# Retention and FFN on one core: four more tiles turned by DMA, mask products and state sums moved to later slots, and the first states kept in their own output bank

## The chip, the core and the metric

The kernel runs on one core of a Trainium2 chip. The metric is the device time of one execution in microseconds (us), shown as the median of several runs. The engines are named as in the profile: PE is the matrix engine (PEld its weight loads), DVE the vector engine, ACT the scalar engine, POOL the general engine (GpSimd), SP the engine that here only issues DMAs. SBUF is the on-chip memory, PSUM the accumulator memory of eight banks.

## The reference, cut to what matters

```python
# q, k, v: (8 batches, 8 heads, 576 positions, 64); w_in (512, 2048); w_out (2048, 512)
scores = scale * np.matmul(q, k.transpose(0, 1, 3, 2))
Dmat = np.where(rel >= 0, gamma[:, None, None] ** rel[None, :, :], 0.0)   # rel = i - j
attn = np.matmul(scores * Dmat[None], v)
x = attn.transpose(0, 2, 1, 3).reshape(8 * 576, 512)
h = x @ w_in
g = np.where(h > 0.0, h, np.exp(np.minimum(h, 0.0)) - 1.0)
out = g @ w_out                                                           # (4608, 512) float32
```

A causal linear attention with a decay per head is followed by a two-layer feed-forward network (FFN) with an ELU between its layers. All matrix products are in bf16 with float32 accumulation.

## The kernel before

The 4608 tokens are cut into 36 units of 128 tokens. Two batches make nine units (`R = 9`); the fifth of each nine holds the end of one batch and the start of the next. The decay factors apart: `gk` scales the rows of v, `gx` the outputs.

**A unit's attention.** `load_v` (SP's queue) and `load_qk` (POOL's queue, cast to bf16 on the way) bring the data in. `scale_v` (POOL) writes `vn`. `turn` makes `qkT`, the transposed q and k: for units below `PE_TURNED = 12` by eight PE transposes into the score bank (tag `sc`), copied out by DVE (q) and ACT (k); from unit 12 on by one DMA transpose from SBUF to SBUF on SP's queue. `scores` (PE, L211) fills the score bank, `masks` (DVE, L223) multiplies it with the triangular mask into `pt`. `inter` (L244, queries times the running state `sb`) and `intra` (L299, `pt` times `vn`) build the unit's output in the bank pair `o`, of which there is one. `put_x` (DVE, L312) multiplies it by `gx` and writes `xt`, the input of the FFN. `state` (PE, L260) computes the unit's own contribution k^T v into the unused half of the `o` bank of the unit before; `state_out` (DVE, L275 to L281, then a cast on ACT) adds it to the running sum and makes the next `sb`. For units 0 to 3, `state_aside` (ACT, L290) first copies the contribution out of PSUM, so that the bank is free.

**The FFN.** Units are gathered in groups of 1 to 4. `ffn1` (L382) makes one 512-wide bank `ph` (three banks, tag `ph`); ACT takes its exp (`e`, L387), POOL forms `m = e - 1` (L389), and DVE writes `g` (L347), the step that frees the bank. That last step is held back in the list `late` and written into the program three slots later by `finish`. `ffn2` (L407, in the start L438) multiplies `g` with w_out into `pm`; ACT copies the result and a DMA writes it out.

**Order.** The schedule is manual: every engine runs its instructions in the order in which the program emits them. The start up to unit 5 is written out by hand, with dummy matmuls (`dummy`, L452) between the first units. Then a list of slots, one per `ffn1` or `ffn2` call (four groups of matmuls), is walked; due times place the calls of unit u between them: `stretch(u)` (scores of u+1, inter and intra of u, state of u+1, then the DVE work), `turn`, `scale_v` and the loads. A unit below 12 is turned and scaled about two units ahead of its stretch, a later one three. `todo` holds calls for later slots; `tick` ends each slot.

The emission of DVE's work in `stretch` before:

```python
        if u == 5:
            finish(2)
        if last:
            put_x(u)
        if ahead:
            masks(u + 1)
        if not last:
            put_x(u)
        if ahead:
            todo.append((slot[0] + 1, lambda: state_out(u + 1, True)))
```

Of the kernel before, what the change touches and what calls it, by code (L numbers as in the profile page):

```python
# [9 lines left out]
FP32 = mybir.dt.float32  # L10
# [7 lines left out]
def kernel(  # L18
# [9 lines left out]
    nc = tc.nc  # L28
    PSUM = bass.MemoryType.PSUM

    B, H, S, D = q.shape
    DM, DF = moe_w_in.shape
    P = 128
    HP = H // 2
    KJ = DM // P
    NFT = DF // P
    NU = B * S // P
# [5 lines left out]
    GROUPS += [list(range(u, u + 4)) for u in range(16, NU, 4)]  # L43
    NG = len(GROUPS)
    group_of = {u: (g, i) for g, us in enumerate(GROUPS) for i, u in enumerate(us)}
    PE_TURNED = 12

    def place(u):

# [114 lines left out]
    def make_gx(*hps):  # L164
        for hp in hps:
            nc.scalar.activation(gx[:, hp, :S], px, AF.Exp, bias=bx, scale=lgx[:, hp : hp + 1])


    qkTs, vns, scs, pts, os_, sbs, sts, sums = {}, {}, {}, {}, {}, {}, {}, {}

# [7 lines left out]
            gk[:, u % R, h0:h1].unsqueeze(2).to_broadcast([P, h1 - h0, D]), ALU.mult,  # L178
        )

    def turn(u, bank=None, keys_on_v=False):

        t = tpool.tile([P, 2, HP, P], BF16, name="qkT", tag="qkT")
        n = kns[u]
        c_v = 1 if keys_on_v else 0
        if u < PE_TURNED:
            if bank:
                pool, tag = bank
                ps = [pool.tile([P, HP, P], BF16, name="tr", tag=tag) for c in range(2)]
            else:  # L190
                both = ps_s.tile([P, 2, 2, HP, P], BF16, name="tr", tag="sc")
                ps = [both[:, c, 0] for c in range(2)]
            for c in range(2):
                for hp in range(HP):
                    nc.tensor.transpose(ps[c][:, hp], n[:, c, 2 * hp : 2 * hp + 2].rearrange("p h d -> p (h d)"), ident)  # L195
            nc.vector.tensor_copy(t[:, c_v], ps[c_v])
            nc.scalar.copy(t[:, 1 - c_v], ps[1 - c_v])  # L197
        else:
            nc.sync.dma_start_transpose(
                t.rearrange("p c h t -> p (c h) t"), n.rearrange("p c h d -> p (c h d)")  # L200
            )
        qkTs[u] = t
# [14 lines left out]
    def masks(u, i=None):  # L217

        if u not in pts:
            pts[u] = ppool.tile([P, 2, HP, P], BF16, name="pt", tag="pt")  # L220
        m = mask[:, 1 if u % R == 4 else 0]
        s = slice(0, 2) if i is None else slice(i, i + 1)
        nc.vector.tensor_tensor(  # L223
            pts[u][:, s].rearrange("p i h t -> p (i h) t"), scs[u][:, s].rearrange("p i h t -> p (i h) t"),
            m.unsqueeze(1).to_broadcast([P, (s.stop - s.start) * HP, P]), ALU.mult,
        )
# [4 lines left out]

    def inter(u):

        o = ps_o.tile([P, 2, 512], FP32, name="o", tag="o")
        os_[u] = o
        r = u % R
        if r == 0:
            return
        n = 64 if r == 4 else P
        for a in range(2):  # L240
            for b in range(2):
                for i in range(2):
                    rows = slice(i * D, (i + 1) * D)
                    nc.tensor.matmul(  # L244
                        o[b * D : (b + 1) * D, i, a * P : a * P + n], sbs[u][rows, 2 * b + a],
                        qkTs[u][rows, 0, 2 * b + a, :n],
                        start=(a == 0), stop=False, skip_group_check=True,
                    )

    def state(u):  # L250

        r = u % R
        if r == 8:
            return
        sts[u] = os_[u - 1][:, 1 if r == 4 else 0, 256:512].rearrange("p (c d) -> p c d", c=HP)
        rows = slice(64, P) if r == 4 else slice(0, P)
        for hp in range(HP):
            for i in range(2):
                h = 2 * hp + i
                nc.tensor.matmul(  # L260
                    sts[u][i * D : (i + 1) * D, hp], kns[u][rows, 1, h], vns[u][rows, h],
                    start=(hp == 0), stop=(hp == HP - 1), skip_group_check=True,
                )

    slot = [0]
    todo = []

    def state_out(u, cast_later=False):
        r = u % R
        if r == 8:  # L270
            return
        s = ppool.tile([P, HP, D], BF16, name="sb", tag="sb")
        sbs[u + 1] = s
        if r in (3, 7):
            nc.vector.tensor_tensor(s, sts[u], sums[u - 1], ALU.add)  # L275
            return
        sums[u] = ppool.tile([P, HP, D], FP32, name="sum", tag="sum")
        if r in (0, 4):
            nc.vector.tensor_copy(sums[u], sts[u])
        else:  # L280
            nc.vector.tensor_tensor(sums[u], sts[u], sums[u - 1], ALU.add)  # L281
        if cast_later:
            todo.append((slot[0] + 1, lambda: nc.scalar.copy(s, sums[u])))  # L283
        else:
            nc.scalar.copy(s, sums[u])

    def state_aside(u):

        c = ppool.tile([P, HP, D], FP32, name="stc", tag="stc")
        nc.scalar.copy(c, sts[u])  # L290
        sts[u] = c

    def intra(u):
        o = os_[u]
# [11 lines left out]
    def put_x(u):  # L306
        g, i = group_of[u]
        if i == 0:
            xts[g] = xpool.tile([P, KJ, 512], BF16, name="xt", tag="xt")
        r = u % R  # L310
        s0 = P * r if r < 5 else 64 + P * (r - 5)
        nc.vector.tensor_tensor(  # L312
            xts[g][:, :, i * P : (i + 1) * P].rearrange("p (a i) t -> p a i t", a=2), outputs(os_[u]),
            gx[:, :, s0 : s0 + P].rearrange("p (a i) t -> p a i t", a=2), ALU.mult,
        )

    def stretch(u, ahead=True):

        ahead = ahead and u + 1 < NU
        if ahead:  # L320
            scores(u + 1)
        inter(u)
        intra(u)
        if ahead:
            state(u + 1)
        last = GROUPS[group_of[u][0]][-1] == u
        if u == 5:
            finish(2)
        if last:
            put_x(u)  # L330
        if ahead:
            masks(u + 1)
        if not last:
            put_x(u)
        if ahead:
            todo.append((slot[0] + 1, lambda: state_out(u + 1, True)))


    gts = {}
# [3 lines left out]
    def finish(n=0):  # L343

        while late and late[0][0] <= slot[0] - n:
            _, gt_, ph, m, _ = late.pop(0)
            nc.vector.scalar_tensor_tensor(gt_, ph, 0.0, m, ALU.max, ALU.min)  # L347
# [98 lines left out]

    V, A, G = nc.vector.tensor_copy, nc.scalar.copy, nc.gpsimd.tensor_copy

    def dummy(n, bank=(ps_m, "pm")):
        dum = bank[0].tile([P, 512], FP32, name="dum", tag=bank[1])  # L450
        for _ in range(n):
            nc.tensor.matmul(dum, warm[:, :P], warm, start=True, stop=True)  # L452

    def product(u):
        inter(u)
        intra(u)
        put_x(u)
# [17 lines left out]
    load_w_out(0, 8)  # L475
    load_w_out(8, 16)
    dummy(2)
    os_[-1] = ps_o.tile([P, 2, 512], FP32, name="o", tag="o")
    for u in range(2):
        scores(u)  # L480
        masks(u)
        if u == 0:
            make_gx(1, 2, 3)
        dummy(1)
        state(u)
        state_aside(u)
        dummy(2)
        turn(u + 1, h, True)
        product(u)
        state_out(u)  # L490
        dummy(2)
# [5 lines left out]
    def f1(g, n, bank=None):  # L497
        k = 512 // (P * len(GROUPS[g]))
        ffn1(g, k * n, bank)

    ffn1_part(0, 0, 0, 2)
    state(2)
    state_aside(2)
    ffn1_part(0, 1, 0, 2)
    product(2)
    state_out(2)
# [11 lines left out]
    for n in range(4, 16):  # L518
        f1(0, n, m if n % 4 == 1 else None)
        if n == 9:  # L520
            turn(3)
        if n in (9, 10):
            scale_v(3, n - 9)
        if n == 11:
            scores(3)
            masks(3, 0)
        if n == 12:
            masks(3, 1)
            state(3)
            state_aside(3)  # L530
        if n == 13:
            product(3)
            state_out(3)
    for n in range(4):
        f1(1, n, m if n == 1 else None)
        if n == 0:
            load_v(4, nc.vector)
    load_qk(4)
    finish()
# [12 lines left out]
    load_v(7, nc.vector)  # L552
    ffn2_part(1, 8, 16, None)
    scores(4)
    state(4)
    masks(4)
    state_out(4)
    scale_v(6)
    ffn2_part(2, 8, 16, None)
    product(4)  # L560
    turn(5)
    load_qk(8)
    load_v(8, nc.vector)
    ffn2_part(3, 8, 16, None)
    scores(5)
    state(5)
    masks(5)
    state_out(5)
    f1(2, 0)
    f1(2, 1)  # L570
    turn(6)
    f1(2, 2)
    load_qk(9)
    load_v(9, nc.vector)
# [30 lines left out]
    for u in range(5, NU):  # L605
        def at(share):
            return due[u] + share * (due[u + 1] - due[u])
        events.append((due[u], 0, u))
        if u + 2 < PE_TURNED:
            events += [(due[u], 3, u + 2), (at(0.7 if u in (5, 7) else 0.5), 1, u + 2)]  # L610
        if PE_TURNED <= u + 3 < NU:
            t = at(0.4) if u + 2 < PE_TURNED else due[u]
            events += [(t, 1, u + 3), (t, 3, u + 3)]
        if u + 5 < NU:
            events += [(at(0.25), 4, u + 5), (at(0.6), 5, u + 5)]
    events.sort()
# [50 lines left out]
```

## Time and profile before

| | before |
|---|---|
| median of 12 runs | 314.97 us (314.05 to 316.79) |
| profiled execution | 314.16 us, span 312.4 us |
| PE busy | 302.1 us, 97% |
| DVE, ACT, POOL busy | 183.1, 127.4, 201.8 us |
| granted PE clock | 1.00 |
| DMA | 39.55 MB, mean 127 GB/s |
| DMA transposes on SP | 24, median 4.4 us from issue to landing |
| PE transposes | 96 matmuls, DVE copies 12 x 422 ns, ACT copies 12 x 585 ns |

The span runs from the first to the last instruction of the profiled execution; the rest of the run's own time lies around it. Busy shares are averages over stages; matmuls overlap, so their mean duration is longer than the distance between two of them. The chain of waits follows the work that ended last back to the start, and shows in order of time what each step stood on.

### The profile page before, as it was taken

The numbers are of one execution on the slowest core, as the hardware profiler recorded it, in microseconds if no ns is written. First come the engines' busy times: TensorE is split into PE (matmuls) and PEld (weight loads), VectorE is DVE, ScalarE is ACT, GpSimd is POOL, SyncE is SP. The second block draws the span as 40 slices with busy tenths as digits, with TensorE's granted clock in tenths as the row PEclk, the third lists the DMA queues.
The fourth block names the chain that finished last, engine by engine and source line by source line (L and its number), as shares of the span: only waits on it lengthen the run. The fifth ranks groups of instructions, "written<-read, shape, count | busy, mean of one in ns | idle before, by whom it ended". The sixth has DMA issues, their size and how long they took to land.

```text
span 312.4 us, 7391 instructions
## 1 busy us (share of the span) xinstructions
PE 302.1 (97%) x2925; PEld 166.7 (53%) x2964; DVE 183.1 (59%) x309; ACT 127.4 (41%) x237; POOL 201.8 (65%) x292
## 2 busy tenths in 40 slices
PE   8899999999999999999999999999999999999996
PEld 3475646777765555555444444444444444444444
DVE  4679425767685766765766665666665665434300
ACT  4556314335534443344344433444344433444411
POOL 8887794978987787797777666766664433333300
PEclk9999999999999999999999999999999999999999
DMA  9999999997899999999999999999995200100112
GB/s 156 189 202 206 169 169 216 180 175 56 107 148 190 134 130 151 155 151 163 114 150 137 135 136 134 136 135 136 135 136 86 67 36 35 36 34 34 64 72 70
DMA packets 146659, 39.55 MB, mean 127 GB/s; under 512 B 137600, under 2 KB 142080, under 8 KB 146624
## 3 DMA queue, kind: packets, MB, share of 16 engines
q0 software_dynamic: 77264, 13.64, 55.8%
q1 hardware_dynamic: 67920, 23.14, 39.3%
q10 hardware_dynamic: 1440, 2.29, 2.1%
q8 instruction: 23, 0.38, 0.5%
q14 instruction: 12, 0.10, 0.1%
HBM read 36.70 MB, written 9.44 MB: 148 GB/s over the span
## 4 chain that ended last, share of the span: by engine, by line
PE 86%; DMA 7%; DVE 3%; issue 2%; POOL 1%; ACT 0%; SPq 0%; DVEq 0%; POOLq 0%
PE ph L382 36%; PE pm L407 34%; DMA w_in_sb<-in_moe_w_in_dram 6%; PE pm L438 4%; PE sc L211 4%; PE o L299 4%; DMA rv<-in_v_dram 2%; PE o L260 1%; PE pmh L423 1%; PE o L244 1%; PE tr L195 1%; DVE g L347 1%; DVE pt L223 1%; DVE xt L312 0%; SPq L114 0%
## 5 line engine op out<-in xcount | busy, mean ns | idle before, releaser
L389 POOL TENSOR_SCALAR m<-e 128x512 bf16<-128x512 f32 (+1 forms) x156 | 90.6, 583 | 91.7 <-ACT e L387 87.0
L382 PE MATMUL ph<-xt,w_in_sb 128*128 128x512 bf16 (+3 forms) x792 | 141.5, 312 | 2.7 <-DVE g L347 1.1
L347 DVE SCALAR_TENSOR_TENSOR g<-ph,m 128x512 bf16<-128x512 f32 (+1 forms) x156 | 99.5, 647 | 67.5 <-POOL m L389 67.0
L387 ACT ACTIVATE e<-ph 128x512 f32<-128x512 f32 (+1 forms) x156 | 87.1, 564 | 125.5 <-PE ph L382 119.0
L407 PE MATMUL pm<-w_out_sb,g 128*128 128x512 bf16 x478 | 122.8, 379 | 1.6 <-issue 1.0
L382 PEld LDWEIGHTS <-w_in_sb 128*128 128x128 bf16 x808 | 68.8, 98 | 54.1 <-issue 2.4
L407 PEld LDWEIGHTS <-g 128*128 128x128 bf16 x496 | 47.8, 98 | 53.0 <-issue 0.3
L223 DVE TENSOR_TENSOR pt<-sc,mask 128x1024 bf16<-128x1024 f32 (+1 forms) x37 | 44.1, 1192 | 19.5 <-PE sc L211 18.4
L176 POOL TENSOR_TENSOR vn<-rv,gk 128x512 bf16<-128x512 f32 (+1 forms) x37 | 37.8, 1022 | 0.2 <-DMA rv<-in_v_dram 0.2
L93 POOL DMA_DIRECT2D qkn<-in_q_dram x39 | 35.1, 899 | 0.5 <-issue 0.4
L93 POOL DMA_DIRECT2D qkn<-in_k_dram x39 | 33.4, 858 | 1.0 <-DMA qkn<-in_k_dram 1.0
L312 DVE TENSOR_TENSOR xt<-o,gx 128x512 bf16<-128x512 f32 x36 | 24.7, 685 | 12.1 <-PE o L260 8.3
L414 ACT COPY ot<-pm 128x512 f32<-128x512 f32 x31 | 18.1, 585 | 13.9 <-PE pm L407 13.9
L211 PEld LDWEIGHTS <-qkT 64*64 64x64 bf16 x576 | 9.2, 106 | 13.9 <-issue 10.6
L211 PE MATMUL sc<-qkT 64*64 64x128 bf16 x576 | 15.0, 222 | 0.6 <-ACT qkT L197 0.2
L299 PE MATMUL o<-pt,vn 128*64 128x128 bf16 x288 | 14.9, 225 | 0.1
L438 PE MATMUL pm<-w_out_sb,g 128*128 128x512 bf16 x61 | 14.2, 379 | 0.2
L197 ACT COPY qkT<-tr 128x512 bf16<-128x512 bf16 x12 | 7.0, 585 | 15.4 <-DVE rv L82 10.7
L283 ACT CAST sb<-sum 128x256 bf16<-128x256 f32 x19 | 7.7, 403 | 11.8 <-DVE sum L281 8.3
L452 PE MATMUL dum<-warm 128*128 128x512 bf16 x26 | 9.8, 501 | 1.2 <-DVE warm L119 1.2
L299 PEld LDWEIGHTS <-vn 128*64 128x64 bf16 x288 | 9.2, 109 | 3.2
L438 PEld LDWEIGHTS <-g 128*128 128x128 bf16 x64 | 6.1, 98 | 6.6
(53 smaller groups left out, 110.1 us busy)
## 6 DMA issues: line engine op xcount, KB each, us to landing
rv<-in_v_dram SPq DMA_DIRECT2D x31, 256.0 KB, 5.1
out_dram<-ot SPq DMA_DIRECT2D x27, 256.0 KB, 2.3
qkn<-in_q_dram POOLq DMA_DIRECT2D x31, 128.0 KB, 4.8
qkn<-in_k_dram POOLq DMA_DIRECT2D x31, 128.0 KB, 5.3
w_in_sb<-in_moe_w_in_dram POOLq DMA_DIRECT2D x8, 256.0 KB, 9.1
w_out_sb<-in_moe_w_out_dram POOLq DMA_DIRECT2D x2, 1024.0 KB, 15.7
out_dram<-ot ACTq DMA_DIRECT2D x8, 256.0 KB, 4.2
rv<-in_v_dram SPq DMA_DIRECT2D x8, 128.0 KB, 6.5
```

Source lines behind the costliest of these rows:

```text
L93: nc.gpsimd.dma_start(kns[u][p0 : p0 + n, c], (q, k)[c][b, :, s0 : s0 + n, :].rearrange("h p d -> p h d"))
L176: nc.gpsimd.tensor_tensor(vns[u][:, h0:h1], raws[u][:, h0:h1], gk[:, u % R, h0:h1].unsqueeze(2).to_broadcast([P, h1 - h0, D]), ALU.mult,)
L211: nc.tensor.matmul(sc[j * 64 : (j + 1) * 64, i, hp], t[r, 1, hp, j * 64 : (j + 1) * 64], t[r, 0, hp], start=(hp == 0), stop=(hp == HP - 1) ...
L223: nc.vector.tensor_tensor(pts[u][:, s].rearrange("p i h t -> p (i h) t"), scs[u][:, s].rearrange("p i h t -> p (i h) t"), m.unsqueeze(1).t ...
L299: nc.tensor.matmul(o[b * D : (b + 1) * D, i, a * P : (a + 1) * P], vns[u][:, h], pts[u][:, i, 2 * b + a], start=(u % R == 0 and a == 0), s ...
L312: nc.vector.tensor_tensor(xts[g][:, :, i * P : (i + 1) * P].rearrange("p (a i) t -> p a i t", a=2), outputs(os_[u]), gx[:, :, s0 : s0 + P] ...
L347: nc.vector.scalar_tensor_tensor(gt_, ph, 0.0, m, ALU.max, ALU.min)
L382: nc.tensor.matmul(ph[:, i * n : (i + 1) * n], w_in_sb[:, j, f : f + P], xts[g][:, j, :n], start=(j == 0), stop=(j == KJ - 1), skip_group_ ...
L387: nc.scalar.activation(e[:, w], ph[:, w], AF.Exp)
L389: nc.gpsimd.tensor_scalar(m[:, w], e[:, w], -1.0, 1.0, ALU.add, ALU.mult)
L407: nc.tensor.matmul(pm, gts[g, ft][:, it * P : (it + 1) * P], w_out_sb[:, ft], start=(ft == 0), stop=(ft == NFT - 1))
L438: nc.tensor.matmul(acc[u], gts[g, ft][:, it * P : (it + 1) * P], w_out_sb[:, ft], start=(ft == 0), stop=(ft == NFT - 1))
```

## The change

- `PE_TURNED` is 8: units 8 to 11 are turned by DMA transposes on SP, placed with their `scale_v` three units ahead. `scale_v(7)` moves into the hand-written start.
- In `stretch`, `put_x` always comes first. From unit 7 on, the mask product is emitted one slot later, and `state_out` two slots later instead of one. `finish(2)` at u == 5 goes. `turn(6)` and `turn(7)` use the share 0.5 or the hand-written place; `state_out(5)` comes after `turn(6)`.
- Units 0 to 3: `state_aside` goes. The state is computed inside `product`, in the unit's own `o` bank, just before inter and intra; `state_out(3)` comes a few FFN calls later.
- In the first two units the dummy matmuls are 3 + u before `turn(u + 1)`, 2 + u between its two halves and 2 behind, instead of 1, 2 and 2.

```diff
-    PE_TURNED = 12
+    PE_TURNED = 8
...
             for c in range(2):
+                if c:
+                    dummy(between)
                 for hp in range(HP):
...
-    def state(u):
+    def state(u, beside):
...
-        sts[u] = os_[u - 1][:, 1 if r == 4 else 0, 256:512].rearrange("p (c d) -> p c d", c=HP)
+        sts[u] = os_[beside][:, 1 if r == 4 else 0, 256:512].rearrange("p (c d) -> p c d", c=HP)
...
         if ahead:
-            state(u + 1)
-        last = GROUPS[group_of[u][0]][-1] == u
-        if u == 5:
-            finish(2)
-        if last:
-            put_x(u)
-        if ahead:
-            masks(u + 1)
-        if not last:
-            put_x(u)
-        if ahead:
-            todo.append((slot[0] + 1, lambda: state_out(u + 1, True)))
+            state(u + 1, u)
+        put_x(u)
+        if u + 2 < PE_TURNED:
+            masks(u + 1)
+        elif ahead:
+            todo.append((slot[0] + 1, lambda: masks(u + 1)))
+        if ahead:
+            todo.append((slot[0] + 2, lambda: state_out(u + 1, True)))
...
-    def product(u):
+    def product(u, with_state=True):
+        os_[u] = ps_o.tile([P, 2, 512], FP32, name="o", tag="o")
+        if with_state:
+            state(u, u)
         inter(u)
         intra(u)
         put_x(u)
...
-        dummy(1)
-        state(u)
-        state_aside(u)
-        dummy(2)
-        turn(u + 1, h, True)
+        dummy(3 + u)
+        turn(u + 1, h, True, 2 + u)
         product(u)
         state_out(u)
         dummy(2)
...
-            state(3)
-            state_aside(3)
         if n == 13:
             product(3)
-            state_out(3)
     for n in range(4):
         f1(1, n, m if n == 1 else None)
         if n == 0:
+            state_out(3)
             load_v(4, nc.vector)
...
     scores(5)
-    state(5)
+    state(5, 4)
     masks(5)
-    state_out(5)
     f1(2, 0)
     f1(2, 1)
     turn(6)
+    state_out(5)
+    scale_v(7)
     f1(2, 2)
...
         if u + 2 < PE_TURNED:
-            events += [(due[u], 3, u + 2), (at(0.7 if u in (5, 7) else 0.5), 1, u + 2)]
-        if PE_TURNED <= u + 3 < NU:
-            t = at(0.4) if u + 2 < PE_TURNED else due[u]
-            events += [(t, 1, u + 3), (t, 3, u + 3)]
+            events.append((at(0.5), 1, u + 2))
+        if u + 3 < NU:
+            events += [(due[u], 1, u + 3), (due[u], 3, u + 3)]
```

In `events`, kind 1 is `turn` and kind 3 is `scale_v`.

More of the change, by code (lines that the diff above doesn't have):

```diff
@@ L166, in make_gx, with dummy @@
             nc.scalar.activation(gx[:, hp, :S], px, AF.Exp, bias=bx, scale=lgx[:, hp : hp + 1])
+    def dummy(n):
+        if n:
+            dum = ps_m.tile([P, 512], FP32, name="dum", tag="pm")
+        for _ in range(n):
+            nc.tensor.matmul(dum, warm[:, :P], warm, start=True, stop=True)
     qkTs, vns, scs, pts, os_, sbs, sts, sums = {}, {}, {}, {}, {}, {}, {}, {}
@@ L179, in scale_v, with turn @@
         )
-    def turn(u, bank=None, keys_on_v=False):
+    def turn(u, bank=None, keys_on_v=False, between=0):
         t = tpool.tile([P, 2, HP, P], BF16, name="qkT", tag="qkT")
@@ L232, in inter @@
     def inter(u):
-        o = ps_o.tile([P, 2, 512], FP32, name="o", tag="o")
-        os_[u] = o
+        if u not in os_:
+            os_[u] = ps_o.tile([P, 2, 512], FP32, name="o", tag="o")
+        o = os_[u]
         r = u % R
@@ L285, in state_out @@
             nc.scalar.copy(s, sums[u])
[L287 to L291, printed above, removed]
     def intra(u):
@@ L447 @@
     V, A, G = nc.vector.tensor_copy, nc.scalar.copy, nc.gpsimd.tensor_copy
[L449 to L452, printed above, removed]
-    def product(u):
+    def product(u, with_state=True):
+        os_[u] = ps_o.tile([P, 2, 512], FP32, name="o", tag="o")
+        if with_state:
+            state(u, u)
         inter(u)
@@ L477 @@
     dummy(2)
-    os_[-1] = ps_o.tile([P, 2, 512], FP32, name="o", tag="o")
     for u in range(2):
@@ L501 @@
     ffn1_part(0, 0, 0, 2)
-    state(2)
-    state_aside(2)
     ffn1_part(0, 1, 0, 2)
@@ L554 @@
     scores(4)
-    state(4)
+    state(4, 3)
     masks(4)
@@ L559 @@
     ffn2_part(2, 8, 16, None)
-    product(4)
+    product(4, False)
     turn(5)
```

## The prediction

> **What bounds the kernel now.** I read the page first (busy shares, slices), then the chain of waits in order of time, then the timeline of the stretches where the chain leaves PE, then the DMA queues' own waits.
>
> The page, rows of busy time, of DMA share in 40 slices of 7.8 us, and of the chain by engine:
>
> ```profile
> PE 302.1 (97%) x2925; PEld 166.7 (53%) x2964; DVE 183.1 (59%) x309; ACT 127.4 (41%) x237; POOL 201.8 (65%) x292
> DMA  9999999997899999999999999999995200100112
> PE 86%; DMA 7%; DVE 3%; issue 2%; POOL 1%; ACT 0%; SPq 0%; DVEq 0%; POOLq 0%
> ```
>
> PE sets the time and the DMA engines are occupied until 240 us. But where? The chain in order of time (start, length, what), once in the second half and then at the start:
>
> ```profile
> 202.12 0.86 PE pm L407 x4
> 202.98 0.35 PE sc L211 x16
> 203.33 0.34 PE o L299 x8
> 203.67 0.12 PE o L260 x8
> 203.80 0.32 PE ph L382
> ...
> 17.59 8.86 DMA w_in_sb<-in_moe_w_in_dram
> 26.45 0.14 issue
> 26.59 0.81 PE ph L382 x4
> ```
>
> From about 125 us the chain holds PE rows alone: four 512-wide matmuls take 0.86 us (0.216 each) and scores, products and state follow with no gap. Nothing that frees DVE, ACT or a PSUM bank there can shorten it, and PE's instructions there stay the same. Before 26.45 us the chain is the load of the last quarter of w_in; PE waits 0.15 us for it. So the change can act between 26.6 and 125 us. There the chain leaves PE at these places:
>
> ```profile
> 59.45 0.46 PE tr L195 x8
> 59.92 0.02 issue
> 59.94 0.44 DVE qkT L196
> 60.38 0.02 issue
> 60.40 0.59 ACT qkT L197
> 60.99 0.04 issue
> 61.04 0.42 PE sc L211 x16
> ...
> 71.39 0.61 DVE g L347
> 72.00 0.05 issue
> 72.05 1.05 PE ph L382 x8
> ...
> 110.85 1.23 DVE pt L223
> 112.07 0.60 DVE xt L312
> 112.67 0.48 DVE g L347
> ```
>
> PE waits for DVE's g, which frees an FFN bank (`ps_h` has three), and g stands behind a mask product (1.23 us) and an x product; at 59.9 scores wait for the two copies that follow a PE transpose.
>
> **Part 1: units 8 to 11 turned by DMA.** Each had eight PE transposes in a chain row of 0.45 to 0.46 us (at 64.76, 70.48, 75.86, 82.45): 4 x 0.455 = 1.82 us off PE, where PE is the chain. The matmul group says 227 ns for one, but they overlap; 0.455/8 = 57 ns is what one costs. The Trainium skill ("TensorE: Matmul & The Clock Gate", Part 4: PE-mode transpose) gives ~390 ns in isolation and ~275 ns within a kernel; by it the 32 would be worth 8.8 us (an estimate), by the row 1.8. The row is this kernel's own, back to back, so it stands. Also gone: four DVE copies (422 ns) and four ACT copies (585 ns); they count only where DVE sets PE, which is part 2.
>
> What it adds: four transposes of 256 KB on SP. The order of the changed program on SP is v(9), T(8), v(10), T(9), v(11), T(10), v(12), T(11), v(13), T(12): where v loads ran ahead to 63 us before, each now stands behind a T, and each T waits for its unit's k. Deadlines, on the clock of before and moved by the sums below from 59 us on: T(u) before scores(u), at 67.0, 72.8, 78.2, 83.4 us; v(u) before scale_v(u) on POOL, at stretch(u-3). Loads of k(8) to k(11) were issued at 48.2, 56.4, 60.4, 65.3 and took 6.9, 7.3, 7.7, 5.7 us. The moved scale_v(7) (1.05 us on POOL) delays k(9) by some 0.4. So T(8) issues at 55.4 with over ten us in hand, and T(9), the tightest, at 64.1. No transpose runs in that stretch before; the nearest row is those from 75 to 129 us:
>
> ```profile
> L199 SPq DMA_TRANSPOSE qkT<-qkn x9: 1239/1326/2337, 75.5 to 128.7; - x9
> ...
> DMA to landing us min/median/max: 4.2/5.0/6.5
> ```
>
> At 5.0 T(9) lands at 69.1, at 6.5 at 70.6, at the longest of the whole trace (8.0) at 72.1: in time. The skill ("Advanced Engine Details and Errata", X-Bar Transpose (TRN2)) says such transposes are as fast as ordinary DMAs, 350 to 400 GB/s: 0.7 us for 256 KB, by which T(9) lands near 67 with 6 us in hand. The trace leaves 2 to 4. v(11) follows at 65.4 to 66.4 and takes 5.4 to 9.1 us (v loads of this stretch): 70.8 to 75.5, due at 72.8, with perhaps 0.6 us of slack on POOL. I take 6 us: no stall. Cost 0; the far end is the slower rival.
>
> **Part 2: masks one slot later, x product always first, sums two slots later.** Losses are read as the real distance in the chain less the PE rows.
> - 110.83: 0.11+0.34+0.12+0.86+1.30 would end at 113.56, the chain has 114.00; with 0.03 in the scores 0.47 lost. In the new order DVE does xt (0.6), g, then pt: g ends near 112.5, before PE wants the bank. Gone: -0.47.
> - 118.62: 0.65+0.86+1.30 would end at 121.43, it is 122.13: 0.70 lost to xt, pt, sb ahead of g. Now xt, g, pt, g, sb: -0.70.
> - 70.94 (after tr(9)): 1.75 us of ph took 2.15: 0.40 lost, g behind a qkT copy that is now gone. But with tr(9) gone PE does four ph groups in a row on three banks. The first starts at 68.74, its exp ends at 70.31, m at 71.01, g would end near 71.7, so the fourth can start 3.04 us after the first; PE needs 2.62. New wait 0.42 + 0.17 for a restart (the 1.05 row against 0.87): +0.59 - 0.40 = +0.19. What is late next is the exp, m, g latency itself.
> - 59.9: masks(6) stay at once, but `finish(2)` at u == 5 is gone, and DVE now does xt, pt, g, g, sum, qkT(7). xt starts near 57.0 (0.2 later, since the sum of state(5) has moved ahead of g at 54): 0.61+1.22+0.65+0.65+0.41+0.44 ends at 61.0 less overlap, about 60.85; the ACT copy (0.59) follows, scores(7) at 61.5, not 61.04: +0.46. PE itself would be there at 61.1.
> - 30.31: eight ph of 0.163 from 29.01 end at 30.31, the next starts at 30.66 behind xt, sb, g. `state_out(3)` moves past g: -0.35. The loads behind it follow POOL's work, which moves along.
> - After 125 us: 0, since the bank waits have slack there. Later sums hold the o bank two slots at most; stretches stand four slots apart or more, so inter(u+1) finds it free.
>
> **Part 3: state in the own bank, no copy aside.** Three ACT copies (364 ns) leave the loop and a fourth goes later; two sums from `stc` (1085 ns mean, one of 1.75) become reads of PSUM (415). Six dummies more: 6 x 0.216 = 1.3 us if PE were the limit. It isn't: PE waits for k(1) and k(2) (0.34 and 0.42 us) and for the copies of qkT, where the dummies sit; what moves behind k's landing is state, 0.12 us each. Then w_in at 26.45 covers it, 0.15 us away. Bounds -0.2 to +1.3; near the first, 0.
>
> **Sum** against the profiled execution (314.16, of which the span is 312.4): -1.82 - 0.47 - 0.70 + 0.19 + 0.46 - 0.35 = -2.69, so 311.5. That execution lies 0.8 under the median of the runs shown (314.97): 312.3 as a median. About 0.3%, 0.94 us, is what a measurement of this kernel can tell from no change.
>
> **Rivals.**
> - *SP's head of line (slower).* T(9) waits for k(9), v(11) stands behind T(9), and POOL, in order, stops at scale_v(11) with the m of group 4 behind it; then g, then the FFN bank. For it: DMA share 1.2 to 1.8 in 55 to 67 us, v loads of up to 9.1 us. Against: the v loads that crowded these us are spread out now. It decides once v(11) lands after 73.4. At 8.0 and 9.1 us it comes at 75.5: 2.1 lost; v(12) and v(13) stand behind T(10), T(11) in the same way, 1 to 1.5 each: -2.7 + 4.6 = +1.9, 316.9. Chance 0.26, of which 0.04 ends at no change.
> - *DVE's wait only moves.* The mask, a slot later, falls before another g: the 1.17 us at 111 and 119 stay: 313.5. For it: DVE is busy 5.0 of the 7 us from 111 on. Against: a g lies between. Chance 0.16 (0.12 faster, 0.04 same).
> - *The dummies are on the path.* PE comes 1.3 late at 26.6: 313.6, with part of the former 314.8. Chance 0.10 (0.04 faster, 0.06 same).
> - That the change does not do what it says is out: the changed program's order has 32 transposes fewer on PE and four more on SP.
>
> **Numbers.** Forecast as summed: 0.48, all faster. Faster 0.48+0.12+0.04 = 0.64; same 0.04+0.04+0.06 = 0.14; slower 0.22. Range: the low end 310.9 drops the two new waits (0.46, 0.59) and some spread; the high end 316.2 reaches into the first rival, about the cost of 3.9 instead of 4.6; near 2 in 10 is left outside. For the likeliest case alone 311.2 to 313.6.
>
> **What would show it.** In the changed profile: scores(12) near 89.4 (90.88 before, less 1.82 and 0.35, plus 0.19 and 0.46); no DVE pt ahead of a g in the chain at 111 and 119; a wait of PE for g near 71.7; scores(7) 5.5 us or more behind scores(6) (5.24 before). Wrong: POOL vn waiting for an rv DMA, or PE sc or PEld waiting for a qkT DMA, between 60 and 85 us; or the first FFN matmul after the w_in load later than 26.8.

## The result: 313.0 us, and the profile after

The changed kernel took 313.0 us (median of 12 runs, 312.12 to 314.01) beside 314.97 us of the kernel before (49 runs on the same chip): a ratio of 0.9932, interval 0.9916 to 0.9947. It is faster by about 2 us; the prediction was 312.3. The profiled execution took 313.43 us, its span 311.7 us, with a granted clock of 1.00. Two executions further down, one of `masks_only` and one of `later_both`, fell into a slower state of the chip and are left out of the medians.

The page of the changed kernel, the rows that answer to those shown of before:

```profile
PE 299.6 (96%) x2899; PEld 164.6 (53%) x2938; DVE 179.2 (57%) x305; ACT 123.7 (40%) x229; POOL 201.9 (65%) x292
DMA  9999999999999999999999999999995400000112
PE 83%; DMA 8%; DVE 3%; issue 2%; POOL 2%; ACT 0%; SPq 0%; POOLq 0%; DVEq 0%; ACTq 0%
```

PE has 26 instructions fewer (32 transposes gone, 6 dummies added), DVE and ACT 3.9 and 3.7 us less work. The bound is the same. The start still stands on the load of w_in (chain of the changed kernel; start, length, what):

```profile
17.93 9.94 DMA w_in_sb<-in_moe_w_in_dram
...
28.00 1.46 PE ph L382 x8
```

**A finer ruler.** The last quarter of w_in landed at 27.87 us here and at 26.45 in the profile of before. A first FFN matmul after 26.8 us was one of the prediction's signs of being wrong, and it came at 28.00. Is that the change? The profiled executions do not tie it to the new start: with the old one the load landed at 26.45, 26.5, 26.5 and 28.8 us, with the new one (ten executions) between 26.3 and 28.0. From the start of scores(5) to the end of PE, by contrast, two executions of the changed kernel took 257.27 and 257.25 us, and the distance from one unit's scores to the next repeats within 0.02 us between kernels that have the same order there. So I compare the starts of scores(k), read from the timeline, and not whole spans. From scores(5) to the end of PE: 259.12 us before, 257.27 after, **-1.85**. Unit by unit, where anything differs (distance from scores(k) to scores(k+1), us):

| k to k+1 | before | after | difference | all parts and all corrections (`best`, below) |
|---|---|---|---|---|
| 6 to 7 | 5.31 | 5.39 | +0.08 | 5.30 |
| 7 to 8 | 5.86 | 5.41 | -0.45 | 5.41 |
| 8 to 9 | 6.13 | 5.86 | -0.27 | 5.26 |
| 9 to 10 | 5.83 | 5.38 | -0.45 | 5.39 |
| 10 to 11 | 5.72 | 5.27 | -0.45 | 5.46 |
| 11 to 12 | 6.24 | 6.59 | **+0.35** | 6.24 |
| 13 to 14 | 7.58 | 7.22 | **-0.36** | 7.22 |
| 14 to 15 | 6.61 | 7.03 | **+0.42** | 6.70 |
| 15 to 16 | 7.23 | 6.89 | -0.34 | 6.89 |
| 16 to 17 | 6.83 | 6.50 | -0.33 | 6.22 |
| 20 to 21 | 6.92 | 6.86 | -0.06 | 6.86 |

Four PE transposes are gone at 0.45 each, as the prediction has it; in 8 to 9 a new wait takes part of that back. Two rows, 11 to 12 and 14 to 15, are slower than before without having been foreseen. The chain of the changed kernel shows what PE waits for at 72 us (the new wait of 8 to 9), at those two and at 118 us; at 111 us only PE is in it:

```profile
71.53 0.70 DVE g L347
72.23 0.04 issue
72.27 1.03 PE ph L382 x8
...
84.93 0.69 DVE xt L316
85.62 1.13 DVE pt L232
86.75 0.60 DVE g L347
87.35 0.34 DVE sum L291
...
87.71 0.02 ACT sb L293
...
88.02 0.59 ACT ot L414
...
88.65 1.02 PE pm L407 x4
...
105.21 1.13 DVE pt L232
106.34 0.33 DVE sum L291
106.67 0.48 DVE g L347
...
107.19 0.81 PE ph L382 x4
...
111.09 0.16 issue
111.25 0.81 PE pm L407 x3
...
118.03 0.69 DVE xt L316
118.72 1.13 DVE pt L232
119.85 0.47 DVE g L347
...
120.37 0.81 PE ph L382 x4
```

At 87.35 the state sum, now two slots later, is the fourth thing in a row on DVE; its cast to `sb` is next on ACT, and behind that cast stands `ot`, the output copy that frees the one `pm` bank: PE's next ffn2 starts at 88.65. At 106.34 the same sum stands on DVE between a mask product and the g that PE waits for. At 118.72 a mask product is still ahead of a g, only the sum is no longer there.

### The profile page after: what moved, and what is told of

Its sections match the earlier page's. It is cut to its first block, busy times and chain, and to the rows that moved or that the text cites. A ratio compares the mean times of both kernels' runs of the same rounds, so it can differ in the third digit from the quotient of the medians.

```text
span 311.7 us, 7337 instructions
## 1 busy us (share of the span) xinstructions
PE 299.6 (96%) x2899; PEld 164.6 (53%) x2938; DVE 179.2 (57%) x305; ACT 123.7 (40%) x229; POOL 201.9 (65%) x292
## 4 chain that ended last, share of the span: by engine, by line
PE 83%; DMA 8%; DVE 3%; issue 2%; POOL 2%; ACT 0%; SPq 0%; POOLq 0%; DVEq 0%; ACTq 0%
PE ph L382 35%; PE pm L407 32%; DMA w_in_sb<-in_moe_w_in_dram 6%; PE pm L438 4%; PE o L303 4%; PE sc L220 3%; DMA rv<-in_v_dram 2%; PE o L270 1%; PE pmh L423 1%; PE o L254 1%; DVE pt L232 1%; DVE g L347 1%; DVE xt L316 1%; PE tr L204 1%; POOL vn L183 1%
## 5 line engine op out<-in xcount | busy, mean ns | idle before, releaser
L173 PE MATMUL dum<-warm 128*128 128x512 bf16 x32 | 10.5, 459 | 1.2 <-DVE warm L119 1.2
L206 ACT COPY qkT<-tr 128x512 bf16<-128x512 bf16 x8 | 4.7, 583 | 13.8 <-DVE rv L82 10.7
L270 PE MATMUL o<-vn,qkn 128*64 128x64 bf16 (+1 forms) x256 | 9.5, 196 | 0.0
```

## The experiments

Each kernel is compared with the kernel before on the same chip; the distance from scores(5) to the end of PE is that of its profiled execution.

**The three parts, each alone, and the whole again.** `turn_only` has the kernel before with

```diff
-    PE_TURNED = 12
+    PE_TURNED = 8
```

and the places of `turn` and `scale_v` that go with it; `masks_only` has x first, the mask product of units 7 and up a slot later and the sums two slots behind (the lines of `stretch`, with `u + 2 < 8` written out), with PE turning kept up to unit 11; `bank_only` has the start with the states in their own bank and its dummies; `after_again` is the changed kernel.

> Only units 8 to 11 are turned by DMA (with scale_v three units ahead, scale_v(7) in the start); masks, state sums and the first units stay as before. Theory (PE time saved): the four chain rows of 0.455 us go, of which tr(9) was followed by a wait that is partly replaced by the wait for exp, m, g on three banks; the waits of DVE at 111 and 119 us stay. Ratio to before 0.994 to 0.996 (-1.3 to -1.9 us). Rival (SP's head of line): PE waits for qkT or POOL waits for rv between 60 and 85 us, ratio 1.000 or more. Rival (the state sums and masks are what paid): ratio 0.998 to 1.001.

> Only the DVE order in stretch is changed (x product first, masks of unit 7 on one slot later, state sums two slots later, finish(2) gone, state_out(5) after turn(6)); units 8 to 11 stay on PE, the first units as before. Theory: the two waits at 111 and 119 us shrink, but from the profile after new ones of 0.3 to 0.4 us stand at 85 (output copy behind the cast of the state), 104 and 118: -0.3 to +0.5 us, ratio 0.999 to 1.002. Rival (as predicted, the waits go and nothing comes): -0.7 us or more, ratio below 0.998.

> Only the first units' state is computed in their own bank, without the copy aside, state_out(3) later, six dummies more. Theory: the wait at 30.3 us goes (-0.35 to -0.6) and the load of w_in hides the rest: ratio 0.998 to 0.999. Rival (the start costs): in the profile after, the last w_in load landed at 27.9 instead of 26.5 us; if that comes from this part and not from the spread between executions, the first FFN matmul after it stands near 28.0 here too and the ratio is 1.001 to 1.004.

> The changed kernel once more, beside the three parts on the same chip, and for a second profile of its start. Theory: ratio 0.992 to 0.995; the sum of the three parts' differences comes within 0.6 us of it. If the late w_in of its first profile was spread, the first FFN matmul after w_in stands between 26.4 and 27.5 us; if it belongs to the kernel, at 27.8 to 28.2 again.

Measured, beside 315.39 us of the kernel before (56 runs):

| | median, us | ratio, interval | scores(5) to end of PE | against before |
|---|---|---|---|---|
| turn_only | 314.25 | 0.9972, 0.9955 to 0.999 | 257.77 | -1.35 |
| masks_only | 315.84 | 1.0015, 1.0 to 1.0031 | 259.84 | +0.72 |
| bank_only | 314.66 | 0.9982, 0.9962 to 1.0002 | 259.10 | -0.02 |
| after_again | 313.57 | 0.9949, 0.9924 to 0.9974 | 257.25 | -1.87 |

Three expectations were missed in part: the ratio of `turn_only` lies above 0.994 to 0.996 (its -1.35 is inside), the +0.72 of `masks_only` lies above +0.5, and the parts do not come within 0.6 us of the whole in the traces. They add up to -0.65 and the whole gives -1.85: 1.2 us is an interaction. (In whole times the parts add up to about -1.4 beside -1.8, a difference that their spread can hide.) The moved masks and sums alone lose. Where? In `masks_only` scores(9) to scores(10) takes 6.75 us, not 5.83. Its chain there:

```profile
75.80 1.14 DVE pt L223
76.95 0.14 issue
77.08 0.61 PE tr L195 x8
```

There is one score bank. PE's transposes of unit 10 need it, and it is free only when the mask product has read the scores; a mask product a slot later makes PE wait for it. A unit that a DMA turns never comes to that bank with a transpose. `turn_only`, on its side, has 5.66 us there and not the 5.38 of the whole: with PE's transposes gone it meets a mask product ahead of x and g:

```profile
75.86 1.23 DVE pt L223
77.09 0.60 DVE xt L312
77.68 0.61 DVE g L347
```

The 0.92 that `masks_only` pays and the 0.28 that `turn_only` pays, both absent in the whole, are the 1.2.

**Masks late only where a DMA turns the next unit.** Is that conflict all of it? With the edit the masks of units 7 to 10 stay at once; that of unit 11 moves, since unit 12 does not come to the score bank.

```diff
-        if u + 2 < 8:
+        if u + 2 < PE_TURNED:
```

> The order part alone, as in masks_only (x product first, sums two slots later, PE turning kept up to unit 11), but with the mask product moved a slot later only for units that a DMA turns (12 and up). In masks_only the PE transposes of unit 10 stood behind a late mask product on the one score bank: +0.93 us at scores(9) to scores(10), and +0.73 from scores(5) to the end of PE (259.84 us against 259.11 before). My theory: that is a conflict of the two parts and belongs neither to the masks nor to the turning alone; here the stretch from scores(9) to scores(10) falls back to 5.7 to 5.9 us, and scores(5) to the end of PE takes 258.3 to 258.9 us. Rival: the cost is that of the later sums or of x ahead of the mask, on whatever unit; then 259.5 or more remains.

315.16 us beside 314.9 (ratio 1.0015, 0.9995 to 1.0035), 259.56 us from scores(5) to the end of PE: slower than my theory's 258.3 to 258.9, and about what the rival asked. From scores(9) to (10) it fell from 6.75 to 6.21, so more than half of the 0.92 was the bank. The chain of this kernel puts the rest, and 6.90 instead of 6.24 from (11) to (12), on the later sum; no run has the late sum without the other moves:

```profile
77.19 0.33 DVE sum L279
77.52 0.34 DVE qkT L196
...
78.36 0.61 ACT e L383
```

A sum two slots later stands ahead of the copy of the PE transpose on DVE, ACT's copy follows that one, and the exp of the FFN is behind both. So both parts of the order (late mask, and by this chain late sum) cost where PE turns. From unit 13 on, where a DMA turns in every kernel here, `masks_only` has the same distances as the whole: the move gains there with or without the DMA transposes of units 8 to 11.

**The new waits: the sum's place.** In the changed kernel:

```diff
-            todo.append((slot[0] + 2, lambda: state_out(u + 1, True)))
+            todo.append((slot[0] + 3, lambda: state_out(u + 1, True)))
```

> The changed kernel with state sums three slots behind the stretch instead of two. The changed kernel has two waits that the kernel before has not: +0.35 us between scores(11) and (12), where the cast to sb stands on ACT behind the sum and ahead of the output copy that frees the one pm bank, and +0.42 between scores(14) and (15), where the sum stands on DVE ahead of a g. Theory: both come from the sum's place and go; scores(5) to the end of PE is 256.5 us instead of 257.26, the whole 0.7 us faster. Rival: DVE and ACT are simply full there, and the next instruction in line gives the same wait, or the sum, a slot later, falls before another g or output copy: 257.1 to 257.6.

312.69 us beside 314.9 (0.9915, 0.9887 to 0.9942); 256.65 us, 0.62 less than the changed kernel. 11 to 12 is back at 6.25, 14 to 15 at 6.70 (7.03), 6 to 7 at 5.31. In 18 to 19 it adds 0.16: the cast to `sb` now meets another output copy. So the sum's place made the whole of the one new wait and 0.33 of the 0.42 of the other; 0.09 at 14 to 15 (6.61 before) stays unexplained, and the rival has the 0.16.

**And the mask one slot later again,** from stretch(14) on:

```diff
-            todo.append((slot[0] + 1, lambda: masks(u + 1)))
+            todo.append((slot[0] + (2 if u >= 14 else 1), lambda: masks(u + 1)))
```

> later_sums, and from stretch(14) on the mask product two slots behind instead of one. Beyond later_sums this takes the mask product (1.13 us) from between x and g at 105 and 120 us. Theory: the rest of the wait between scores(16) and (17), about 0.3 us, and any rest of that between (14) and (15) go: scores(5) to the end of PE 256.1 us. Rival: in groups of three units pt comes too late for intra or stands before the next g: scores 14 to 17 as in later_sums or later, 256.5 to 257.2.

311.31 us (0.9896, 0.9866 to 0.9927; five executions); 256.38 us, 0.28 above the 256.1 expected. 16 to 17 goes from 6.50 to 6.22, the 0.28 that the mask product at 118.72 still cost. 14 to 15 does not move.

**The wait at 72 us.** PE runs four FFN banks in a row on three banks. In the changed kernel an ffn2 call is moved in between:

```diff
-            if b * len(f1s) <= a * len(f2s) and b < len(f2s) or a >= len(f1s):
+            if b * len(f1s) <= (a + (g == 4)) * len(f2s) and b < len(f2s) or a >= len(f1s):
```

> The changed kernel with one ffn2 call of group 3 put after the third instead of the fourth ffn1 of group 4, so that PE does not run four FFN banks in a row with the three it has. Theory: the wait for g at 72 us (e 0.60, m 0.61, g 0.69 in a row from the end of the first bank) goes: scores(8) to scores(9) 5.3 to 5.5 us instead of 5.86, scores(5) to the end of PE 256.7 to 256.9 instead of 257.26. Rival: four of the eight calls before the next stretch still wait for DVE, which has xt, pt and two g to do there, so that the wait moves to the next bank or to the pm bank: scores(8) to scores(9) 5.7 us or more.

312.23 us (0.9909, 0.9885 to 0.9932); 256.85 us. 8 to 9 falls from 5.86 to 5.26: 0.60, where the prediction had put this wait at 0.59. 10 to 11 gives back 0.17 (5.27 to 5.44).

**All of them, and the best version.** `all_three` has the three edits above; `best` has in addition `slot[0] + (3 if u < 16 else 2)` for the sums.

> The changed kernel with all of later_both (sums three slots behind, masks two from stretch(14) on) and f2_earlier. later_both measured 256.38 us from scores(5) to the end of PE, f2_earlier 0.42 less than the changed kernel's 257.27. If the two don't touch each other: 255.96. f2_earlier lost 0.17 of its 0.61 again between scores(10) and (11); if that is the sum that stands ahead of a g there, it goes with later sums: 255.8. Rival: parts of this schedule act on each other again, as the turning and the masks did, and give back 0.4 or more: 256.4 or above.

> all_three, but sums three slots behind only up to stretch(15), two from stretch(16) on. With later sums the cast to sb came ahead of an output copy on ACT between scores(18) and (19): 6.57 us there against 6.41. Theory: that 0.16 goes and nothing else moves: 0.16 less than all_three from scores(5) to the end of PE, 255.6 to 255.8, and about 1.1 per cent faster than the kernel before. Rival: at the border, between scores(16) and (18), two sums come close to each other and cost 0.2 or more.

| | median, us (before 315.04) | ratio, interval | scores(5) to end of PE |
|---|---|---|---|
| all_three | 312.25 | 0.9914, 0.9892 to 0.9935 | 255.97 |
| best | 312.28 | 0.991, 0.9894 to 0.9927 | 255.82 |

Here the edits add (255.97 for 255.96 expected) and the border costs nothing: 18 to 19 is 6.41 again. The 0.17 between scores(10) and (11) stays, so the sum is not its cause; the chain of `all_three` has one restart of PE there, after 0.01 us at 79.51, 0.05 us behind the end of a g. `best` is 3.30 us shorter than before and 1.45 shorter than the changed kernel where the traces can be compared. In medians it is about 2.8 us below before (0.9 per cent, not the 1.1 expected), and no different from `later_both` (0.9896) or `f2_earlier` (0.9909): the last tenths drown in the spread of the loads at the start, where the profiled `best` waited for k(4) until 44.5 us.

**The slack of the DMA transposes.** In the changed kernel they are given out two units ahead instead of three:

```diff
-            events += [(due[u], 1, u + 3), (due[u], 3, u + 3)]
+            events += [(due[u], 1, u + 3), (due[u], 3, u + 3)] if u + 3 >= 12 else [(due[u], 3, u + 3)]
+        if 8 <= u + 2 < 12:
+            events.append((at(0.0), 1, u + 2))
```

> The changed kernel with the DMA transposes of units 8 to 11 given out two units ahead of their stretch instead of three: each stands one v load later in SP's queue. This takes the slack that the prediction counted on. In the changed kernel T(8) to T(11) were issued at 56.5, 64.3, 67.6 and 71.9 us and landed at 62.9, 70.2, 74.5, 78.4, needed at 67.4, 73.2, 78.6, 83.9: 3 to 5.5 us in hand. Theory: T(8) then is issued at 60 to 62 and T(9) at 66 to 68, they take 5.5 to 7 us and PE waits for one or both, 0.5 to 2.5 us in all, with PE sc behind DMA qkT in the chain at 67 to 75; scores(5) to the end of PE 257.8 to 259.8, the gain of the change half or wholly gone. Rival: SP is not held up by the v loads, the issue moves under 2 us, and nothing changes: 257.2 to 257.4.

313.47 us (0.9953, 0.9934 to 0.9973), 257.26 us: nothing changed, every distance is that of the changed kernel. Counted from scores(5), T(8) to T(11) were issued at 5.7, 13.4, 17.7 and 22.4 us instead of 5.4, 13.2, 16.5 and 20.8. My theory fell: one place in SP's queue is not what sets their time. SP's own waits in the changed kernel between 50 and 85 us (for what; us in all, times, longest) say what does:

```profile
SPq L208 <- DMA qkn<-in_k_dram: 11.4, 6, 5.2
SPq L84 <- DVE rv L82: 9.7, 2, 5.0
```

A transpose mostly waits at the head of the queue for its k to land (11.4 us in six waits); to stand one place further back cost 0.2 to 1.6 us of issue. They still landed 2.0 to 4.0 us ahead of their scores.

**Twelve dummies more.** Six more in each of the first two units, `dummy(9 + u)` for `dummy(3 + u)`:

> The changed kernel with six dummy matmuls more in each of the first two units (12 x 0.216 = 2.6 us if PE set the time there). The prediction put the six that the change adds at nothing, because the load of the last quarter of w_in ends later than PE's work. Theory: covered; the first FFN matmul after that load starts 0.13 to 0.15 us behind its landing, and from that landing to scores(5) it takes 23.3 us as in the changed kernel (23.26). Rival: PE has no room before 26 us: 24.5 to 26 us from the landing to scores(5), or a chain that goes over PE instead of the w_in load.

313.33 us (0.9941, 0.992 to 0.9961). From the landing of w_in to scores(5) it takes 23.43 us; the load lands at 27.55 and the FFN starts at 27.68 behind it. 2.6 us of additional PE work leave no trace in the time: the cover holds for the six dummies of the change, with room for twelve more.

## Why the prediction was right, and where not

The sign and the main mechanisms hold (transposes off PE, waits for g shortened, one new wait at 72 us), and the range held the time. The size came out at about three quarters: from scores(5) on the prediction had -2.34 of its -2.69, and -1.85 was measured. Of the -0.35 that it put before scores(5) the run times show nothing: the medians fall by 1.97 here and 1.82 in `after_again`, about what scores(5) to the end of PE gives alone. That the sum came so near is in part luck, since errors cancel: 0.38 less for scores(7) and 0.36 unforeseen at 13 to 14 on one side, 0.77 of new waits and 0.5 at 111 and 118 on the other. Luck too is that scores(12), one of the prediction's signs, came 1.17 us earlier, counted from scores(5), exactly as summed: 0.38 too little at scores(7) met 0.35 unforeseen at 11 to 12.

| step of the prediction | predicted | measured |
|---|---|---|
| four PE transposes at 0.455 | -1.82 | -0.45 in each of four stretches, 8 to 9 net of its wait |
| 8 to 9: new wait less the old one | +0.19 | +0.18 (-0.27 instead of -0.45) |
| scores(7) behind DVE's backlog | +0.46 | +0.08 |
| wait at 110.83 | -0.47 | -0.34 |
| wait at 118.62 | -0.70 | -0.33; the other 0.28 only in `later_both` |
| state_out(3) past g | -0.35 | about -0.5 from w_in to scores(5), none in the run times |
| dummies, SP's queue, after 125 us | 0 | 0, 0, -0.06 |
| not in the prediction | 0 | -0.36 at 13 to 14, +0.35 at 11 to 12, +0.42 at 14 to 15 |

**The transposes.** 57 ns for one, from the chain row, was the right price: `turn_only` has -0.45 in 7 to 8 and 10 to 11 as well. By the 275 ns of the Trainium skill's "TensorE: Matmul & The Clock Gate" (Part 4: PE-mode transpose) each stretch would have lost 2.2 us (an estimate, 8 x 275 ns); the row, back to back, decides.

**SP's head of line.** The slower rival did not come. Transposes in the changed kernel, from the trace: issued at 56.50, 64.32, 67.62, 71.94, landed at 62.91, 70.18, 74.46, 78.35, and needed at 67.38, 73.24, 78.62, 83.89. The prediction had T(9) issued at 64.1 and took 6 us for it: 64.32 and 5.87. v(11) landed at 72.23, and POOL read it at 74.67; between 60 and 85 us no `vn` waits for v and no scores for a transpose. This is also where a figure misleads: by the skill's "Advanced Engine Details and Errata", X-Bar Transpose (TRN2), a 256 KB transpose at 350 to 400 GB/s takes 0.7 us (an estimate), so that T(9) would have landed near 64.8 (the prediction's "near 67" does not follow from its own 64.1). Here it takes 5.9 to 6.8 us from issue to landing, where the profile's DMA digits are 9. The same section's "as fast as regular DMAs" is not far off: v(11), as large, took 5.4 us beside it. A bandwidth was read as the time of one transfer. The transposes were in time because they were issued early enough, not because they are fast: 3 to 5.5 us in hand, and 2.0 to 4.0 in `late_turn`.

**scores(7), +0.46, came to +0.08.** The prediction made DVE's copy of unit 7's q end at 60.85 on the clock of before, 61.7 on that of the changed profile (scores(6) is 0.85 later in it). The trace has it start at 60.88 and end at 61.29. DVE's queue is as written, but it began 0.2 earlier, at 57.62, and each of five instructions overlaps the one behind it by about 0.08 us, of which the prediction took off only part. The forecast wait all but vanishes because the copies just make it: ACT's ends at 61.91 and PE reads at 61.97. `later_sums`, which puts the sum behind that copy, removes the 0.08.

**The waits at 111 and 119.** At 111 the wait is gone from the chain. The gain is 0.13 smaller than forecast because the price was a difference of row sums, and without the wait the ffn2 call at 111.25 takes 0.97 us with the issue ahead of it (0.16 + 0.81), not the 0.86 of the sum: 0.11 of the 0.13. At 118 the foreseen order xt, g, pt, g, sb is not what came: it is xt, pt, g. Before, the chain had there

```profile
118.65 0.69 DVE xt L312
119.34 1.13 DVE pt L223
120.47 0.33 DVE sb L275
120.80 0.47 DVE g L347
```

so that only the sum is gone from in front of the g. One slot later is not late enough for the mask product there, so in that place the rival "DVE's wait only moves" holds in part (0.28, by `later_both`). What failed in this step is the reading that the mask, a slot later, lies behind the g in both places.

**What was missed.** The prediction followed the sum's move only to where it helps (30 and 119 us), not to where it arrives. "DVE is busy 5.0 of the 7 us" was in it, but the two places where a sum two slots later meets a g or an output copy were not looked for: +0.77. And it did not read the smallest waits of before as prices. In the chain of the kernel before:

```profile
99.14 0.66 PE ph L382 x4
99.81 0.01 issue
99.82 0.82 PE ph L382 x4
```

and of the changed kernel in the same place, all eight together:

```profile
98.81 1.30 PE ph L382 x8
```

At 99.81 the timeline has PE's weight load wait for DVE's g, which came behind a mask product:

```profile
97.95 1.21 DVE L223 TENSOR_TENSOR pt<-sc,mask 128x1024 bf16<-128x1024 f32 x1
99.08 0.68 DVE L347 SCALAR_TENSOR_TENSOR g<-ph,m 128x512 bf16<-128x512 f32 x1
99.81 0.44 PEld L382 LDWEIGHTS <-w_in_sb 128*128 128x128 bf16 x4 [0.41 <-DVE g L347]
```

In the changed kernel that g runs at 97.61, ahead of the mask product: the move that the prediction priced at 111 worked here too. PE itself stood still for 0.01 us, and the four matmuls after it took 0.82 us instead of 0.65; the same again at 102.16 (0.01 and 0.81), where the profile names no releaser. That is 0.35 in all, and in the changed kernel neither wait is there. Two lines that looked like rounding were worth as much as a wait at 111.

**The start.** From the last quarter of w_in to scores(5), in executions whose chain runs over that load: 23.84 and 23.79 us with the old start (before, `masks_from_12`), 23.25 to 23.55 with the new one (eight executions, middle 23.3). That is about -0.5 for the -0.35 of state_out(3); what the rest is was not separated. But the run times do not show it. `bank_only` alone gives 0.7 us in medians, with an interval that just reaches no change. Over the ten kernels with the new start (85 executions), what is left of the run times' difference from before, once each profile's change from scores(5) on is taken off, is -0.04 us in the mean, to about 0.25 either way. So the wait at 30.3 us is gone and is worth nothing that these runs can tell; whether later landings of w_in or waits for k(4) take it back stays open.

## What to carry to other kernels

A late place for an instruction is free only if you know what stands behind it in the new place: list for each moved instruction the two or three that follow it on its engine and who waits for those, before crediting the place that it left. Changes to an order that share a single bank or an in-order queue need not add up; here the late masks and sums lost 0.7 us alone and brought 0.5 once the transposes of units 8 to 11 had left the score bank. Where the loads at the start spread by 1 to 2 us, compare the distance between two landmarks of the bounding engine, which repeats to hundredths, not whole runs.

## What the runs showed of the hardware that was not expected

- In these chains a wait of PE for a g costs 0.16 to 0.18 us more than its own length, even when it is 0.01 us long: it lengthened the next four matmuls from 0.65 to 0.82 (before, at 99.82), and in `all_three` the next eight from 0.87 to 1.05 (at 79.52). After a long wait the row is the same (0.81 for four at 113.19 before).
- SP is held longer by the issue of one 256 KB DMA transpose (1.34, 2.39, 3.52 and 1.93 us for T(8) to T(11); median 1.34 over the 28 of the changed kernel) than by that of a v load (0.37 to 1.10 us, median 0.55).
- In the profiled executions (granted clock 0.998 to 1.00) the spread lies in the loads. Where the order is the same, the distances from scores(5) on repeat within 0.02 us, while the last quarter of w_in lands anywhere from 26.3 to 28.8 us.
